# Attention and gated MLP on one core: the Y heads' tokens rotated by 64 partitions and loaded in three transfers, so that sums and values of X and Y heads stand in the same columns

## The chip, the cores and the metric

The kernel runs on one core of a Trainium2 chip. The metric is the device time of one execution in microseconds (us). Before the change, eight executions have a median of 317.72 us, between 315.1 and 320.2.

The engines are named as the profile names them: PE is TensorE's matmul and PEld its weight load, DVE is VectorE, ACT is ScalarE, POOL is GpSimd, SP is SyncE. SP has no arithmetic here; it issues transfers. A name with a q (SPq, POOLq) is an engine's queue.

## The reference

There are 8 batches of 12 heads, 448 tokens and 64 elements a head. Attention comes first, and its output, the heads side by side (768 wide), goes into a gated MLP that mixes tokens.

```python
def rmsnorm(x, g):
    rms = np.sqrt(np.mean(x * x, axis=-1, keepdims=True) + 1e-06)
    return x / rms * g
q_n, k_n = (rmsnorm(q, g_q), rmsnorm(k, g_k))
scores = scale * np.matmul(q_n, k_n.transpose(0, 1, 3, 2))
attn = softmax(scores)
x = (attn @ v), heads side by side

h = np.maximum(x @ w_in, 0.0)
u, v = h[..., :512], h[..., 512:]
v_n = (v - mean(v)) / np.sqrt(var(v) + 1e-06)
v_s = np.einsum('ts,bsd->btd', w_spatial, v_n) + b_spatial[None, :, None]
out = (u * v_s) @ w_out
```

The last five lines and the line with softmax are shortened here. All inputs and the output are float32; the kernel computes most of its products in bfloat16.

## The kernel before, in words

**Tiling of q, k and v.** A partition is one of 128 rows of on-chip memory. 448 tokens are three and a half times 128. The kernel pairs heads 0 to 5 (the X heads) with heads 6 to 11 (the Y heads), so that two heads fill seven chunks of 128 rows: a q or k tile is 128 partitions x 6 heads x 7 chunks x 64 elements. Of each head, tokens 0 to 383 are the main part (partition p, chunk c holds token 3p + c) and tokens 384 to 447 the tail. An X head has its main part in chunks 0 to 2 and its tail in the lower 64 partitions of chunk 3. A Y head has its tail in the upper 64 partitions of chunk 3 and its main part in chunks 4 to 6. So a batch's q takes four transfers (`load_main` and `load_tail`, lines 94 to 106, each for X and Y), k as many. v is kept per head in four chunks, with the half of chunk 3 that a head does not use set to zero (lines 165 and 166); it is loaded by POOL with four transfers a batch (`load_v`).

**Order of the tokens.** After the transposes the tokens of an X head stand as main, tail, and those of a Y head as tail, main. Scores are made key chunk by key chunk (`scores`), and chunk 3 holds 64 keys of an X head and 64 of a Y head.

**A group.** The three groups g of a batch have four heads each: X heads g and 3 + g, Y heads 6 + g and 9 + g. 24 groups run in order; two of their seven score chunks make a step. In each step ScalarE takes the exponential of both (L358). Squares, their sums, the root and the scaling of q and k (L234, L242, L250 and L251, L261) are made some steps ahead by a table of steps written by hand (`EVEN`, `ODD`, `FIRST`, `todo`). From group 6 on, q and k are transposed by transfers that SP issues (L325), and VectorE then multiplies k by the two weights (`k_scale`, L331).

**Attend.** When a group's exponentials are there, `attend` (line 403) makes three sums on TensorE with `weigh` (L379): part -1 with ones, which are the sums of the exponentials, and parts 0 and 1, the two halves of the 64 value columns. A sum of 4 heads x 32 rows fills 128 partitions of one bank of PSUM, the matmuls' output memory; there are four banks in `ps_w` for these and all MLP sums. X heads are written to columns 64 to 511 of the bank and Y heads to columns 0 to 447, so that both have their main part in columns 64 to 447. The tails are then in different columns for the upper and the lower partitions, which is why whatever reads the bank works in three parts (`PARTS`): the main part on 128 partitions x 384 columns, and two tails of 64 x 64. `recip` (L391, L392) takes the logarithm in these three parts and one exponential of its negative, which gives the reciprocal sums rc. `xt_store` (L401) multiplies each half by rc, again in three parts, into xt, the transposed attention output.

**The MLP** of a batch is cut into pieces of a few matmuls (`unit_v`, `unit_u`, `unit_s`, `unit_o`: L465, L495, L505, L537) that `fill` deals out between the scores, a batch later, so that each step gets an equal share. Their results leave PSUM by VectorE or ScalarE (L434, L436, L440, L442, L509).

**Queues.** Every engine works in the order in which the program gives it its instructions. SP issues all q and k loads after the first few, the DMA transposes and the output stores. In the program each of these transfers waits until the one issued eight before it has landed. For batches from 2 on, the loads are entered into `todo` at steps that line 702 gives; a load waits until the tile of two batches before is free.

Of the kernel before, what the change touches and what calls it, by code (L numbers as in the profile page):

```python
# [12 lines left out]
AF = mybir.ActivationFunctionType  # L13
ALU = mybir.AluOpType
# [5 lines left out]
def kernel(  # L20
# [24 lines left out]
    P = 128  # L45
# [38 lines left out]
    def load_tile(b, i):  # L84
        pl = qb_pools[(b + 1) % 2] if b else first
        t = pl.tile([P, 2 * NG, NCH, D], FP, name="kb" if i else "qb")
        qbs[b, i] = t.rearrange("p h c d -> p h (c d)")
        for g in range(NG):
            x = t.rearrange("p (h g) c d -> p h g c d", g=NG)[:, :, g]
            raw[NG * b + g, i] = x  # L90
            if b == 0 and g == 0:
                raw[0, i, 0], raw[0, i, 1] = x[:, :, 0:4], x[:, :, 4:NCH]

    def load_main(b, i, y, g=None, eng=sync):
        c0 = 256 * y
        hs = slice(0, 6) if g is None else slice(g, 6, NG)
        eng.dma_start(out=qbs[b, i][:, hs, c0:c0 + 192], in_=main((q, k)[i][b][6 * y:6 * y + 6][hs]))

    def load_tail(b, i, y, eng=sync):
        eng.dma_start(out=qbs[b, i][64 * y:64 * y + 64, :, 192:256],  # L100
                      in_=tail((q, k)[i][b][6 * y:6 * y + 6]))

    def load_part(b, i, part):
        if part == 0:
            load_tile(b, i)
        (load_main if part < 2 else load_tail)(b, i, part % 2)

    vts = [const.tile([P, H, 4, D], BF, name=f"vt{i}") for i in range(2)]

    def load_v(b, parts):  # L110
        t = vts[b % 2].rearrange("p h c d -> p h (c d)")
        for i in parts:
            y, hs = i % 2, slice(6 * (i % 2), 6 * (i % 2) + 6)
            if i < 2:
                pool.dma_start(out=t[:, hs, 0:192], in_=main(v[b][hs]))
            else:
                pool.dma_start(out=t[64 * y:64 * y + 64, hs, 192:256], in_=tail(v[b][hs]))

    load_tile(0, 0)
    load_tile(0, 1)  # L120
    load_main(0, 0, 0, 0)
    load_main(0, 1, 0, 0, act)
    load_tail(0, 0, 0)
    load_tail(0, 1, 0, act)
    load_tail(0, 0, 1)
    load_tail(0, 1, 1, act)
# [234 lines left out]
    def et_of(G, i, h):  # L361
        s, a = divmod(NCH * G + i, 2)
        return ets[s][:, 2 * a + h, :]
# [4 lines left out]
    def weigh(G, part):  # L368
        b, g = divmod(G, NG)
        vt = vts[b % 2]  # L370
        ps = ps_w.tile([P, 512], FP, name="ps")
        for r in range(4):
            for l in range(4):
                y, h = divmod(l, 2)
                if part < 0:
                    w = ones_t[:, y, :] if r == 3 else ones
                else:
                    w = vt[:, 3 * l + g, r, 32 * part:32 * part + 32]
                pe.matmul(out=ps[32 * l:32 * l + 32, 64 - 64 * y:64 - 64 * y + S], lhsT=w, rhs=et_of(G, 3 if r == 3 else r + 4 * y, h),  # L379
                          start=(r == 0), stop=(r == 3), tile_position=(0, 32 * l))  # L380
        pst[G, part] = ps


    PARTS = ((slice(0, P), slice(64, S), slice(0, SM)), (slice(0, 64), slice(S, 512), slice(SM, S)),
             (slice(64, P), slice(0, 64), slice(SM, S)))

    def recip(G):
        rc = r_pool.tile([P, S], FP, name="rc")
        ps = pst.pop((G, -1))
        for r, i, o in PARTS:  # L390
            act.activation(out=rc[r, o], in_=ps[r, i], func=AF.Ln, bias=0.0, scale=1.0)  # L391
        act.activation(out=rc, in_=rc, func=AF.Exp, bias=0.0, scale=-1.0)  # L392
        rec[G] = rc

    def xt_store(G, half):
        b, g = divmod(G, NG)
        if g == 0 and half == 0:
            xts[b] = x_pool.tile([P, 6, S], BF, name="xt")
        ps = pst.pop((G, half))
        for r, i, o in PARTS:  # L400
            dve.tensor_tensor(out=xts[b][r, 2 * g + half, o], in0=ps[r, i], in1=rec[G][r, o], op=ALU.mult)  # L401

    def attend(G):
        for part in (-1, 0, 1):
# [225 lines left out]
    def early(p):  # L630
        if p == 0:
            transpose_first(0, 1, dve)
            transpose_first(1, 1, dve)
            reduce(1, 0)
        elif p == 3:
            rstd(1)
            scaled(1, 0, eng=dve)
            scaled(1, 1, eng=dve)
            after((1, 1))
            load_v(0, range(4))  # L640
# [24 lines left out]
        if 10 <= p <= 13:  # L665
            attend_late(0, p - 10)
        if 15 <= p <= 18:
            attend_late(1, p - 15)
        if p in (0, 1, 2, 3, 4, 7, 8, 9, 14):
            dummies(6)  # L670
# [29 lines left out]
                        todo.setdefault(s, []).append((what, G, i))  # L700
    for b in range(2, B):
        first_q = {2: S0, 3: 16}.get(b, (21 * b - 36) // 2)
        for n in range(4):
            todo.setdefault(first_q + n // 2, []).append(("ld", NG * b, n))
            todo.setdefault(first_q + 2 + (n if b % 2 == 0 and b > 2 else n // 2), []).append(("ld", NG * b, n + 4))

    ORDER = ("red", "rstd", "sc", "sq", "turn", "tr", "ks", "ld")

    def prep(s, early_act):
        for what, G, i in sorted(todo.get(s, ()), key=lambda x: (ORDER.index(x[0]), x[1:])):  # L710
            if (what == "rstd") != early_act:
                continue
            if what == "ld":
                load_part(G // NG, *divmod(i, 4))
            elif what == "turn":
                transpose_pe(G, i, dve)
            elif what == "sq":
                squares(G, i, eng=act if (G, i) in ((6, 1), (7, 1)) else None)
            elif what == "red":
                reduce(G, i)  # L720
            elif what == "rstd":
                rstd(G)
            elif what == "sc":
                scaled(G, i, eng=dve if (G, i) in ((4, 0), (5, 0)) else None)
            elif what == "tr":
                transpose_dma(G, i)
            elif what == "ks":
                k_scale(G)
# [16 lines left out]
    for s in range(S0, NST):  # L745
        scores(pss[:, 0:2], 2 * s)
        scores(pss[:, 2:4], 2 * s + 1)
        prep(s, True)
        expo(pss, 2 * s, 2)
        prep(s, False)  # L750
        flush()
        if s in v_step:
            load_v(*v_step[s])
        if s == 11:
            load_v(1, range(4))
        if s == 13:
            load_w_sp()
        if s == 21:
            load_w_out()
        if s in gate_step:  # L760
            b = gate_step[s]
            gated(b)
            nxt = min(x for x in list(gate_step) + [NST] if x > s)
            n = sum(1 for x in range(s, nxt - 1) if x not in busy)
            rate = sum(w[0] for w in work) / (n + 0.5)
        if s in busy:
            attend([G for G in range(NGT) if attend_step(G) == s][0])
            quota[0] = 0
        else:
            quota[0] = 0 if s + 1 in busy else 1  # L770
            fill(rate)
# [45 lines left out]
```

## Time and profile before

| what | value |
|---|---|
| median of 8 executions | 317.72 us (315.1 to 320.2) |
| profiled execution, its own time | 316.79 us |
| its span | 315.0 us |
| mean granted clock of TensorE | 0.973 of full speed |
| transfers | 97058 packets, 49.99 MB, mean 159 GB/s |
| the page's chain that ended last | PE 35%, DVE 22%, ACT 15%, POOL 11%, DMA 8%, issue 7% |

The page and the other views come from one execution. Busy time is the time in which an engine had an instruction under way. In the views by group, "idle before" is what the engine stood still ahead of these instructions, and the arrow names what ended most of it. The chain that ended last is followed back from the last instruction, at each step to what released it; "issue" in it is time for which the profile shows no wait. TensorE's matmuls overlap, so a busy TensorE is not one at its peak.

Two figures on transfers: a q or k load of a main part is 576 KB and of a tail 96 KB; their median time from issue to landing is 6.1 us and 5.7 us for q, 7.4 us and 6.0 us for k.

### The profile page before, as it was taken

Reading aid. Unit: us, or ns where it says so; the run is one execution under the profiler, and the core shown is the slowest. Engines: PE = TensorE matmul, PEld = TensorE weight load, DVE = VectorE, ACT = ScalarE, POOL = GpSimd, SP = SyncE. Lnnn points to the kernel's source line nnn. Section 1 sums busy time; section 2 is a strip of 40 time slices with the busy share of each in tenths; the row PEclk is TensorE's granted clock in tenths of the full one; section 3 lists DMA queues with packets and bytes.
Section 4 is the critical chain, followed back from the end, with each engine's and each line's share of the span. In section 5 each row is a group of like instructions: output and inputs, shape, how many; then the busy total and the mean of one; then the engine's idle time right before and its main releaser. Section 6 shows DMA issues by size and latency. Waiting matters only on the chain.

```text
span 315.0 us, 6518 instructions
## 1 busy us (share of the span) xinstructions
PE 277.5 (88%) x2541; PEld 125.9 (40%) x2541; DVE 225.4 (72%) x456; ACT 213.0 (68%) x308; POOL 198.1 (63%) x177
## 2 busy tenths in 40 slices
PE   7488878888969999889988999889989998899995
PEld 7244333433324344334333343334333343444552
DVE  3865866978588759868868958958967956755552
ACT  2678966885758877766867787586777786564411
POOL 3349599589983997469765996399658930400310
PEclk9789979996999999999999999999999999999999
DMA  7989999539999699949899499939530891121135
GB/s 192 323 188 158 257 208 141 155 57 207 166 208 225 155 211 238 284 56 192 145 240 215 45 210 289 220 61 238 88 65 20 83 225 50 27 100 52 25 152 176
DMA packets 97058, 49.99 MB, mean 159 GB/s; under 512 B 66562, under 2 KB 93379, under 8 KB 97027
## 3 DMA queue, kind: packets, MB, share of 16 engines
q1 hardware_dynamic: 74258, 40.71, 56.2%
q0 software_dynamic: 21424, 8.27, 24.2%
q10 hardware_dynamic: 1344, 0.59, 0.7%
q8 instruction: 20, 0.33, 0.5%
q14 instruction: 12, 0.09, 0.1%
HBM read 38.55 MB, written 11.01 MB: 157 GB/s over the span
## 4 chain that ended last, share of the span: by engine, by line
PE 35%; DVE 22%; ACT 15%; POOL 11%; DMA 8%; issue 7%; SPq 1%; ACTq 0%; POOLq 0%; DVEq 0%
ACT et L358 9%; PE ps L537 9%; PE ps L505 6%; DVE xt L401 6%; PE ps L465 5%; PE pss L351 5%; POOL sqt L234 5%; PE ps L379 5%; DVE ms L242 4%; DMA kb<-in_k_dram 4%; POOL n L261 3%; DVE s L473 3%; DMA w_out<-in_moe_w_out_dram 3%; ACT rc L391 2%; PE ps L495 2%
## 5 line engine op out<-in xcount | busy, mean ns | idle before, releaser
L358 ACT ACTIVATE et<-pss 128x1792 bf16<-128x1792 f32 x74 | 123.0, 1662 | 44.9 <-PE pss L351 43.3
L401 DVE TENSOR_TENSOR xt<-ps,rc 128x384 bf16<-128x384 f32 x144 | 43.6, 330 | 46.2 <-ACT rc L392 44.7
L242 DVE TENSOR_REDUCE ms<-sqt 128x14 f32<-128x896 f32 x46 | 49.4, 1077 | 9.5 <-POOL sqt L234 9.0
L537 PE MATMUL ps<-w_out,gt 128*128 128x384 bf16 (+1 forms) x256 | 49.6, 328 | 4.6 <-DVE osb L442 1.9
L465 PE MATMUL ps<-w_in_v,xt 128*128 128x512 bf16 (+1 forms) x192 | 47.6, 381 | 1.5 <-DVE xt L401 1.2
L351 PE MATMUL pss<-qT,kT 64*128 64x448 bf16 x254 | 38.2, 361 | 10.7 <-ACT et L358 5.8
L379 PE MATMUL ps<-et,vt 128*32 128x448 bf16 x768 | 42.7, 360 | 2.5 <-ACT rc L391 2.5
L495 PE MATMUL ps<-xt,w_in_u 128*128 128x448 bf16 x192 | 40.6, 353 | 2.4 <-DVE osb L442 1.8
L261 POOL TENSOR_TENSOR n<-kb,rs 128x896 bf16<-128x896 f32 x22 | 38.6, 1755 | 4.1 <-issue 3.3
L483 POOL TENSOR_SCALAR nm<-mv 128x4 f32<-128x4 f32 x8 | 1.8, 223 | 62.5 <-DVE mv L474 53.0
L261 POOL TENSOR_TENSOR n<-qb,rs 128x896 bf16<-128x896 f32 x18 | 30.5, 1693 | 13.8 <-ACT rs L251 12.7
L234 POOL TENSOR_TENSOR sqt<-qb 128x896 f32<-128x896 f32 x21 | 36.1, 1722 | 0.1
L234 POOL TENSOR_TENSOR sqt<-kb 128x896 f32<-128x896 f32 x21 | 35.4, 1684 | 0.6 <-DMA kb<-in_k_dram 0.5
L537 PEld LDWEIGHTS <-gt 128*128 128x128 bf16 (+1 forms) x256 | 23.4, 100 | 26.1 <-issue 8.6
L442 DVE COPY osb<-ps 128x384 f32<-128x384 f32 (+1 forms) x50 | 26.6, 554 | 8.7 <-PE ps L537 7.8
L505 PE MATMUL ps<-w_spT,vn 128*128 128x448 bf16 (+1 forms) x128 | 29.1, 371 | 0.7 <-DVE xt L401 0.5
L379 PEld LDWEIGHTS <-vt 128*32 128x32 bf16 x768 | 20.9, 99 | 19.8 <-issue 5.7
L487 POOL TENSOR_SCALAR vn<-vs,nm,rv 128x512 bf16<-128x512 bf16 (+1 forms) x32 | 24.1, 766 | 6.1 <-ACT rv L482 3.6
L351 PEld LDWEIGHTS <-kT 64*128 64x128 bf16 x276 | 10.6, 94 | 41.0 <-issue 29.0
L465 PEld LDWEIGHTS <-xt 128*128 128x128 bf16 (+1 forms) x192 | 17.1, 100 | 23.7 <-issue 6.5
L495 PEld LDWEIGHTS <-w_in_u 128*128 128x128 bf16 x192 | 17.2, 98 | 23.1 <-issue 9.3
L473 DVE BATCH_NORM_STATS2 s<-vs 128x6 f32<-128x512 bf16 (+1 forms) x32 | 21.7, 679 | 1.0 <-ACT vs L434 0.8
(85 smaller groups left out, 334.3 us busy)
## 6 DMA issues: line engine op xcount, KB each, us to landing
out_dram<-osb SPq DMA_DIRECT2D x24, 384.0 KB, 4.9
qb<-in_q_dram SPq DMA_DIRECT2D x14, 576.0 KB, 6.1
kb<-in_k_dram SPq DMA_DIRECT2D x14, 576.0 KB, 7.4
vt<-in_v_dram POOLq DMA_DIRECT2D x16, 288.0 KB, 5.7
qb<-in_q_dram SPq DMA_DIRECT2D x16, 96.0 KB, 5.7
kb<-in_k_dram SPq DMA_DIRECT2D x14, 96.0 KB, 6.0
out_dram<-osb SPq DMA_DIRECT2D x7, 192.0 KB, 4.0
qb<-in_q_dram SPq DMA_DIRECT2D x6, 192.0 KB, 4.6
```

Of the source, the lines that this page charges most:

```text
L234: pool.tensor_tensor(out=t, in0=x, in1=x, op=ALU.mult)
L242: dve.tensor_reduce(out=sqs[gk][:, key[1], :], in_=sqt.pop(key).rearrange("p h c d -> p (h c) d"), axis=AX.X, op=ALU.add)
L261: (eng or pool).tensor_tensor(out=t.rearrange("p c h d -> p h c d"), in0=raw[key], in1=rst[gk][:, key[1], :].rearrange("p (h c) -> p h c", ...
L351: pe.matmul(out=ps[:, h, 0:S], lhsT=kT[r, c0:c0 + 128], rhs=qT[r, :], start=True, stop=True, tile_position=(64 * h, 0))
L358: act.activation(out=ets[s][:, 2 * a:2 * a + 2 * m, :], in_=ps[:, 0:2 * m, 0:S], func=AF.Exp, bias=0.0, scale=1.0)
L379: pe.matmul(out=ps[32 * l:32 * l + 32, 64 - 64 * y:64 - 64 * y + S], lhsT=w, rhs=et_of(G, 3 if r == 3 else r + 4 * y, h), start=(r == 0), ...
L401: dve.tensor_tensor(out=xts[b][r, 2 * g + half, o], in0=ps[r, i], in1=rec[G][r, o], op=ALU.mult)
L465: pe.matmul(out=ps[0:m, :], lhsT=xts[b][:, j, t0:t0 + m], rhs=w_in_v[:, j, :], start=(j == 0), stop=(j == 5), tile_position=(0, 0))
L473: dve.bn_stats(out=s6[0:m, :], in_=vs[b][c][0:m, :])
L495: pe.matmul(out=ps[:, 0:S], lhsT=w_in_u[:, j, 128 * f:128 * f + 128], rhs=xts[b][:, j, :], start=(j == 0), stop=(j == 5))
L505: pe.matmul(out=ps[:, 0:S], lhsT=vn_t[b % 2][0:kp, c, 128 * f:128 * f + 128], rhs=w_spT[0:kp, c, :], start=(c == 0), stop=(c == NT - 1))
L537: pe.matmul(out=ps[o:o + m, 0:384], lhsT=gts[b][f][:, t0:t0 + m], rhs=w_out[:, f, r], start=(f == 0), stop=(f == 3), tile_position=(0, o))
```

## The change

The Y heads' tokens are turned by 64 partitions. In chunk 3 the upper 64 partitions now hold the first 64 rows of the main part's first column of tokens, and each later chunk holds the other half of one column and the first half of the next; the tail ends up in the upper half of chunk 6. Read chunk after chunk, the tokens of a Y head thus stand in the same order as those of an X head: main, tail. A Y head's main part takes two transfers of 64 partitions, so a tensor takes five transfers in place of four; bytes and run lengths stay. v is loaded in the same way and its Y heads use the lower zeros in chunk 0.

All sums are written to columns 0 to 447, so `PARTS` goes: `recip` makes one logarithm in place of three, and `xt_store` one product for each half in place of three. The steps of the loads are laid out anew for five parts (q and k one after the other, three or four in a step), and the v loads of a batch are spread over five steps in place of four.

```diff
-    def load_main(b, i, y, g=None, eng=sync):
-        c0 = 256 * y
-        hs = slice(0, 6) if g is None else slice(g, 6, NG)
-        eng.dma_start(out=qbs[b, i][:, hs, c0:c0 + 192], in_=main((q, k)[i][b][6 * y:6 * y + 6][hs]))
...
+    def pieces(x):
+
+        m, t = main(x), tail(x)
+        return ((slice(0, P), 0, 3, m), (slice(0, 64), 3, 1, t), (slice(64, P), 0, 3, m[0:64]),
+                (slice(0, 64), 1, 3, m[64:P]), (slice(64, P), 3, 1, t))
+
+
+    def load_part(b, i, part, g=None, eng=sync):
+        if part == 0 and (b, i) not in qbs:
             load_tile(b, i)
-        (load_main if part < 2 else load_tail)(b, i, part % 2)
+        y, hs = int(part > 1), slice(0, 6) if g is None else slice(g, 6, NG)
+        r, c, n, x = pieces((q, k)[i][b][6 * y:6 * y + 6][hs])[part]
+        c += 3 * y
+        eng.dma_start(out=qbs[b, i][r, hs, D * c:D * (c + n)], in_=x)
...
+            hs = slice(6, 12) if i > 1 else slice(0, 6)
+            r, c, n, x = pieces(v[b][hs])[i]
+            pool.dma_start(out=t[r, hs, D * c:D * (c + n)], in_=x)
+
+    load_part(0, 0, 0, 0)
+    load_part(0, 1, 0, 0, act)
+    load_part(0, 0, 1)
+    load_part(0, 1, 1, None, act)
+    load_part(0, 0, 2, 0)
+    load_part(0, 1, 2, 0, act)
     act.preload_act_table_set("natural_log_exp_and_others")
-    load_main(0, 0, 1, 0)
-    load_main(0, 1, 1, 0, act)
+    load_part(0, 0, 3, 0)
+    load_part(0, 1, 3, 0, act)
+    load_part(0, 0, 4)
+    load_part(0, 1, 4, None, act)
     for g in (1, 2):
         for i in (1, 0):
-            load_main(0, i, 0, g)
-            load_main(0, i, 1, g)
-    for n in range(8):
-        load_part(1, *divmod(n, 4))
+            for part in (0, 2, 3):
+                load_part(0, i, part, g)
+    for n in range(10):
+        load_part(1, *divmod(n, 5))
...
-        dve.memset(t[0:64, 6:12, 3, :], 0.0)
+        dve.memset(t[0:64, 6:12, 0, :], 0.0)
...
-                    w = vt[:, 3 * l + g, r, 32 * part:32 * part + 32]
-                pe.matmul(out=ps[32 * l:32 * l + 32, 64 - 64 * y:64 - 64 * y + S], lhsT=w, rhs=et_of(G, 3 if r == 3 else r + 4 * y, h),
+                    c = (3, 0)[y] if r == 3 else r + y
+                    w = vt[:, 3 * l + g, c, 32 * part:32 * part + 32]
+                pe.matmul(out=ps[32 * l:32 * l + 32, 0:S], lhsT=w, rhs=et_of(G, 3 if r == 3 else r + 4 * y, h),
...
-        for r, i, o in PARTS:
-            act.activation(out=rc[r, o], in_=ps[r, i], func=AF.Ln, bias=0.0, scale=1.0)
+        act.activation(out=rc, in_=pst.pop((G, -1))[:, 0:S], func=AF.Ln, bias=0.0, scale=1.0)
...
-        for r, i, o in PARTS:
-            dve.tensor_tensor(out=xts[b][r, 2 * g + half, o], in0=ps[r, i], in1=rec[G][r, o], op=ALU.mult)
+        dve.tensor_tensor(out=xts[b][:, 2 * g + half, :], in0=pst.pop((G, half))[:, 0:S], in1=rec[G],
+                          op=ALU.mult)
...
-        for n in range(4):
-            todo.setdefault(first_q + n // 2, []).append(("ld", NG * b, n))
-            todo.setdefault(first_q + 2 + (n if b % 2 == 0 and b > 2 else n // 2), []).append(("ld", NG * b, n + 4))
+        for n in range(10):
+            todo.setdefault(first_q + n // (3 if b > 2 else 4), []).append(("ld", NG * b, n))
...
-            v_step.update({s + 6 + i: (b + 2, [i]) for i in range(4)})
+            v_step.update({s + 6 + i: (b + 2, [i]) for i in range(5)})
```

More of the change, by code (lines that the diff above doesn't have):

```diff
@@ L92, in load_tile @@
                 raw[0, i, 0], raw[0, i, 1] = x[:, :, 0:4], x[:, :, 4:NCH]
-    def load_main(b, i, y, g=None, eng=sync):
-        c0 = 256 * y
-        hs = slice(0, 6) if g is None else slice(g, 6, NG)
-        eng.dma_start(out=qbs[b, i][:, hs, c0:c0 + 192], in_=main((q, k)[i][b][6 * y:6 * y + 6][hs]))
[L99 to L104, printed above, removed]
+    def pieces(x):
[4 more added lines that the diff above has]
+        if part == 0 and (b, i) not in qbs:
             load_tile(b, i)
-        (load_main if part < 2 else load_tail)(b, i, part % 2)
+        y, hs = int(part > 1), slice(0, 6) if g is None else slice(g, 6, NG)
+        r, c, n, x = pieces((q, k)[i][b][6 * y:6 * y + 6][hs])[part]
+        c += 3 * y
+        eng.dma_start(out=qbs[b, i][r, hs, D * c:D * (c + n)], in_=x)
     vts = [const.tile([P, H, 4, D], BF, name=f"vt{i}") for i in range(2)]
@@ L112, in load_v @@
         for i in parts:
[L113 to L126, printed above, removed]
+            hs = slice(6, 12) if i > 1 else slice(0, 6)
[7 more added lines that the diff above has]
+    load_part(0, 1, 2, 0, act)
     act.preload_act_table_set("natural_log_exp_and_others")
-    load_main(0, 0, 1, 0)
-    load_main(0, 1, 1, 0, act)
+    load_part(0, 0, 3, 0)
+    load_part(0, 1, 3, 0, act)
+    load_part(0, 0, 4)
+    load_part(0, 1, 4, None, act)
     for g in (1, 2):
         for i in (1, 0):
-            load_main(0, i, 0, g)
-            load_main(0, i, 1, g)
-    for n in range(8):
-        load_part(1, *divmod(n, 4))
+            for part in (0, 2, 3):
+                load_part(0, i, part, g)
+    for n in range(10):
+        load_part(1, *divmod(n, 5))
     ident = const.tile([P, P], BF)
@@ L377, in weigh @@
                 else:
-                    w = vt[:, 3 * l + g, r, 32 * part:32 * part + 32]
-                pe.matmul(out=ps[32 * l:32 * l + 32, 64 - 64 * y:64 - 64 * y + S], lhsT=w, rhs=et_of(G, 3 if r == 3 else r + 4 * y, h),
+                    c = (3, 0)[y] if r == 3 else r + y
+                    w = vt[:, 3 * l + g, c, 32 * part:32 * part + 32]
+                pe.matmul(out=ps[32 * l:32 * l + 32, 0:S], lhsT=w, rhs=et_of(G, 3 if r == 3 else r + 4 * y, h),
                           start=(r == 0), stop=(r == 3), tile_position=(0, 32 * l))
         pst[G, part] = ps
-    PARTS = ((slice(0, P), slice(64, S), slice(0, SM)), (slice(0, 64), slice(S, 512), slice(SM, S)),
-             (slice(64, P), slice(0, 64), slice(SM, S)))
     def recip(G):
         rc = r_pool.tile([P, S], FP, name="rc")
-        ps = pst.pop((G, -1))
-        for r, i, o in PARTS:
-            act.activation(out=rc[r, o], in_=ps[r, i], func=AF.Ln, bias=0.0, scale=1.0)
+        act.activation(out=rc, in_=pst.pop((G, -1))[:, 0:S], func=AF.Ln, bias=0.0, scale=1.0)
         act.activation(out=rc, in_=rc, func=AF.Exp, bias=0.0, scale=-1.0)
@@ L398, in xt_store @@
             xts[b] = x_pool.tile([P, 6, S], BF, name="xt")
-        ps = pst.pop((G, half))
-        for r, i, o in PARTS:
-            dve.tensor_tensor(out=xts[b][r, 2 * g + half, o], in0=ps[r, i], in1=rec[G][r, o], op=ALU.mult)
+        dve.tensor_tensor(out=xts[b][:, 2 * g + half, :], in0=pst.pop((G, half))[:, 0:S], in1=rec[G],
+                          op=ALU.mult)
     def attend(G):
@@ L639, in early @@
             after((1, 1))
-            load_v(0, range(4))
+            load_v(0, range(5))
             load_w_in(1)
@@ L713, in prep @@
             if what == "ld":
-                load_part(G // NG, *divmod(i, 4))
+                load_part(G // NG, *divmod(i, 5))
             elif what == "turn":
@@ L754 @@
         if s == 11:
-            load_v(1, range(4))
+            load_v(1, range(5))
         if s == 13:
```

## The prediction

> **What bounds the kernel now.** I read the page's busy times first. No engine is at its limit over the whole span, TensorE comes nearest:
>
> ```profile
> PE 277.5 (88%) x2541; PEld 125.9 (40%) x2541; DVE 225.4 (72%) x456; ACT 213.0 (68%) x308; POOL 198.1 (63%) x177
> ```
>
> From 126 us on the kernel repeats every two batches (68.5 us), so I asked next for busy time by stretch, cut where the chain of waits changes its engine. Columns: stretch, its length, busy us (instructions) of PE, PEld, DVE, ACT, POOL, clock, DMA share, GB/s.
>
> ```profile
> 104.00:126.65 22.65, 21.73 (x216) 8.94 (x208) 17.09 (x33) 17.64 (x26) 20.18 (x15) 1.00 1.10 199
> 126.65:144.50 17.85, 15.22 (x128) 6.37 (x127) 13.16 (x30) 12.76 (x19) 11.53 (x11) 1.00 0.74 153
> 144.50:171.40 26.90, 24.48 (x217) 10.26 (x221) 22.70 (x46) 18.17 (x25) 19.09 (x17) 1.00 1.04 214
> 171.40:195.10 23.70, 23.01 (x240) 9.99 (x238) 17.47 (x34) 18.83 (x26) 21.65 (x16) 1.00 0.93 169
> ```
>
> TensorE idles 2.63 us in the second line, 2.42 in the third, 0.69 in the fourth: the last is bound by TensorE, the two before it are not. The chain of waits (start, us, what) says by what:
>
> ```profile
> 162.69 0.48 ACT rc L391 x2
> 163.16 0.01 issue
> 163.18 0.23 ACT rc L391
> 163.41 0.02 issue
> 163.43 0.58 ACT rc L392
> ...
> 164.04 0.68 DVE xt L401 x2
> 164.72 0.01 issue
> 164.73 0.23 DVE xt L401
> ...
> 169.75 1.07 DVE kT L331 x2
> 170.83 0.05 issue
> 170.87 0.55 PE pss L351 x4
> ```
>
> VectorE takes its work in order. It waits for the reciprocal sums of a head group, then scales the two halves of the result, then does what is queued behind: copies, sums of squares, and the k scaling (L331) on which the next scores (L351) depend. Each attend is thus a serial piece ScalarE, VectorE, TensorE. What it consists of, grouped by form (line, engine, operation, tiles, shapes, count | busy us, mean ns | idle before):
>
> ```profile
> L401 DVE TENSOR_TENSOR xt<-ps,rc 128x384 bf16<-128x384 f32 x48 | 26.7, 557 | 45.5 <-ACT rc L392 44.7
> L401 DVE TENSOR_TENSOR xt<-ps,rc 64x64 bf16<-64x64 f32 x96 | 20.8, 217 | 0.7
> ...
> L391 ACT ACTIVATE rc<-ps 128x384 f32<-128x384 f32 x24 | 11.6, 485 | 0.8 <-PE ps L379 0.8
> ...
> L391 ACT ACTIVATE rc<-ps 64x64 f32<-64x64 f32 x48 | 10.3, 215 | 0.3
> ```
>
> A 64x64 piece has a sixth of the columns of a main piece and costs 0.4 of its time; there are two for each main piece.
>
> [...] The trace has no engine count, but 64-partition loads land in 5.7 to 6.0 us against 6.1 to 7.4 for the 576 KB ones[...].
>
> **The change part by part.**
>
> *Scaling (L401).* Each half: two 64x64 pieces go, the main piece grows from 384 to 448 columns. Price of a 128x448 product from PSUM: 557 + 64 x 1.06 = 625 ns; the row of gt (L509, same shape) has 620. 48 x (557 + 2 x 217 - 620) = 17.8 us of VectorE busy. The timeline shows the six of an attend in 1.88 us; two of gt stand there in 1.16 to 1.2. So 0.68 us an attend.
>
> *Logarithm (L391).* Three become one of 448 columns: 485 + 64 x 0.84 = 538 ns, which is also the mean of us (L434, same shape). The three take 0.81 us in the timeline, so 0.27 us an attend; 24 x (485 + 430 - 538) = 9.0 us of ScalarE busy.
>
> Both lie one behind the other: up to 0.95 us for each of 24 attends.
>
> *Steady part, 104 to 287 us.* In 126.65 to 144.5 one attend is fully on the chain and a second for half of its scaling, after which TensorE is late: I take 1.2 us of the 2.63 idle. In 144.5 to 171.4 two attends are on it, 1.9 us; the idle is 2.42, and behind the VectorE chain stand waits that do not get shorter (sums of squares from POOL to VectorE to ScalarE's logarithm, L250), so 1.4. In the TensorE stretch 0.2. Together 2.8 of 68.5 us, 7.5 us over 183 us. The stretch 104 to 126.65 shows that TensorE runs at 96% at best (21.73 of 22.65); I take four fifths: **-6.0 us**, bounds -2 and -10.
>
> *Matmuls.* Counts, widths and order are the same on TensorE; the write begins at column 0 of the bank in place of 0 or 64. No row shows a cost for that; I take nothing.
>
> *Loads on SP.* A tensor takes five transfers in place of four (batch 0: three for each later group in place of two), bytes and runs unchanged. In the steady part each issue is 0.6 to 0.7 us of SP, and each transfer waits for the eighth before it. SP waits 89 us for POOL's n before transposes, so there is room. Behind the loads stand the DMA transposes of q and k and the stores. For k the smallest gap I found between landing and use is 3.4 us (issued at 181.91, 5.4 us to land, used by L331 at 190.70); two more issues are 1.3 us, 2.6 with their waits. Cost nothing; if the gap is used up, see the rivals.
>
> *k loads moved one to two steps earlier.* For batch 3 the first, largest k piece goes ahead of two transposes that kept it back until 72.06 us. Chain there: k landed at 81.3, POOL's squares waited 0.55 us for it, and w_out, issued by POOL at 83.92, kept TensorE waiting 1.49 us at 91.95. Four v pieces ahead of w_out cost 0.93 + 3 x 0.70 in place of 3.2 us. So w_out leaves 0.7 us earlier, and up to 0.65 more from the scaling at 58 us, where VectorE is 97% busy. With four attends in 57 to 104: **-1.5 us**, bounds 0 and -4. The far end has the clock drop in it: at 72 to 74 us TensorE worked 0.70 of 2 us, partly waiting for xt (0.75 and 0.55), and ran at 0.50 until 80. Ten matmuls at 0.39 in place of 0.19 us and two score groups at 0.93 in place of 0.55 are 2.7 us that a shorter wait may spare. I do not count on it.
>
> *Start, 0 to 57 us.* The first piece of work needs 98 KB of long runs in place of 98 KB of short ones: 0.3 us earlier. The q loads of group 1 come behind three more issues and the eight-deep limit: landed at 10.6 us, now about 12.4, where ScalarE takes them at 11.39. That is 1 us on ScalarE, but VectorE's n at 13.92 waits behind a sum until then anyway: nothing, at most +1. POOL issues a fifth v piece: 895 ns for the 128-partition piece, 703 for each 64-partition one with 384 runs, so 895 + 4 x 703 against 2 x 895 + 2 x 703, +0.51 us each. At 21.6 us it moves the last v piece from about 28.5 to 29.2, where TensorE starts on v at 28.27: +0.6. At 47 us POOL is busy without a gap: +0.5. The two attends there give back 0.3. Start: **+0.8 us**, bounds -0.4 and +2.2. Later v pieces lie beside POOL's idle time (15.5 us of waits for rs, mv and ps between 126.65 and 195.1).
>
> *End.* After 287.3 us TensorE waits for the last xt, 0.86 us on its weight load. The scaling ends 0.95 us earlier, TensorE then has its own earlier matmuls to finish: **-0.4 us**, bounds -0.2 and -0.9.
>
> Sum: -6.0 - 1.5 + 0.8 - 0.4 = -7.1 us. The profiled execution took 316.79 us (span 315.0 and 1.8 around it), which gives 309.7; the median of the eight runs is 0.93 above that execution, which gives 310.6. I say **310.0**.
>
> **Rivals.**
> *Smaller, TensorE takes over at once:* the stretches with 91% busy TensorE may hold hidden waits inside the modelled matmul ends. For it: 171.4 to 195.1 and 104 to 126.65 are TensorE's already. Against it: 5 us of idle in each 68.5. Then -2 in the steady part and nothing at 57 to 104: 317 - 1.6 = 315.5.
> *Larger:* most of the 0.95 us counts at 20 attends, and the clock drop goes. -10 - 4 + 0.5 - 0.5 gives 303.
> *Slower, the SP queue:* ten transfers a batch in place of eight, eight in flight, smaller ones. At batches 5 and 7 nine loads stand before a q transpose, at 4 and 6 three; a load that waits for a lane holds transposes and stores behind it. It decides once the k transposes come over 3.4 us later: then kT is late, then the scores, then ScalarE's exponentials. At 2 us past that for each of the six batches: +12 - 8 = +4, 321. For it: the two k loads at 192.69 already took 2.51 us to issue. Against it: SP has nothing to do from 169 to 179 us, and mostly waits for POOL before a q transpose.
>
> **How the numbers follow.** Main case 0.60 (307 to 313.5), smaller 0.20 (313.5 to 318), larger 0.09 (302 to 307), slower 0.11. A measurement of this kernel tells 0.5%, 1.6 us, from no change. Of the smaller case 0.09 falls within that, so faster 0.80, same 0.09, slower 0.11. The range 304 to 316.5 leaves out the slower case, most of the no-change case and the far end of the larger one.
>
> **What would show it.** L401 with 48 instructions near 620 ns and L391 with 24 near 538; VectorE busy near 208 us, ScalarE near 204; the period of two batches near 66 us; TensorE idle less in the VectorE stretches and not in its own; POOL's v issues up by about 4 us in all. Wrong: k scaling or scores waiting for a transpose; TensorE waiting for v near 28 us by over 1 us; VectorE's wait for rc growing by what the scaling saves, which would mean that the slot was only moved.

## The result and the profile after

The changed kernel takes **312.96 us** (median of 11 runs, 312.21 to 316.35) against 318.12 us (median of 32 runs, 315.1 to 321.55) for the kernel before; the ratio is 0.9868 with a 95% interval of 0.9836 to 0.9901. Some executions of a kernel fall into a slower state, and this ratio, like every one below, leaves them out, so it is not the quotient of the medians. The forecast was 310.0 with a range of 304 to 316.5. The kernel became faster, as said, by 5.2 us between the medians and by 4.2 us by the ratio (1.32% of 318.12), where 7.7 were forecast. Between the two profiled executions the span went from 315.0 to 311.0 us, which is 4.0 us where the sum of the steps had 7.1.

First the page's row of busy times, of the changed kernel:

```profile
PE 278.6 (90%) x2541; PEld 129.1 (42%) x2541; DVE 208.6 (67%) x360; ACT 205.9 (66%) x260; POOL 202.0 (65%) x185
```

VectorE has 96 instructions and 16.8 us less, ScalarE 48 instructions and 7.1 us less; TensorE has the same 2541 instructions (278.6 in place of 277.5 us). The groups by form show the merged instructions at their forecast prices (620 and 538 ns), and the two that touch v:

```profile
L393 DVE TENSOR_TENSOR xt<-ps,rc 128x448 bf16<-128x448 f32 x48 | 27.9, 618 | 42.3 <-ACT rc L386 37.4 <-PE ps L379 4.8
...
L385 ACT ACTIVATE rc<-ps 128x448 f32<-128x448 f32 x24 | 12.9, 538 | 0.8 <-PE ps L379 0.8
...
L116 POOL DMA_DIRECT2D vt<-in_v_dram x40 | 29.3, 739 | 0.0
...
L379 PE MATMUL ps<-et,vt 128*32 128x448 bf16 x768 | 46.3, 379 | 5.2 <-DMA vt<-in_v_dram 3.5 <-ACT rc L385 1.7
```

POOL's v issues went from 25.5 to 29.3 us in all, as forecast. The last row holds the first surprise: TensorE waited 3.5 us for v. In the kernel before, v was not among what it waited for there:

```profile
L379 PE MATMUL ps<-et,vt 128*32 128x448 bf16 x768 | 42.7, 360 | 2.5 <-ACT rc L391 2.5
```

Next the stretches of two batches, cut at the same reciprocals as the three stretches that the prediction shows (126.65 to 195.10 there). Columns: stretch, length, busy us (instructions) of PE, PEld, DVE, ACT, POOL, clock, DMA share, GB/s.

```profile
130.65:147.40 16.75, 15.07 (x137) 6.88 (x130) 12.26 (x22) 12.14 (x17) 11.28 (x11) 1.00 1.06 182
147.40:172.70 25.30, 23.86 (x213) 10.01 (x211) 20.88 (x36) 17.78 (x21) 19.71 (x18) 1.00 1.06 193
172.70:195.93 23.23, 22.69 (x238) 10.09 (x236) 16.21 (x27) 18.05 (x20) 22.28 (x17) 1.00 1.10 198
```

The period is 65.28 us in place of 68.45. The three stretches are shorter by 1.10, 1.60 and 0.47 us; TensorE's idle time in them went from 2.63, 2.42 and 0.69 to 1.68, 1.44 and 0.54. That is 2.08 of the 3.17 us; the other 1.09 come off TensorE's busy time with the same work, which suggests that some waiting had been counted as busy (the profile models the ends of matmuls: 16 of L379 stand in 0.94 us, at a median of 353 ns for one). The chain of waits (start, us, what) at the same place as in the prediction says why:

```profile
162.74 1.66 ACT et L357
164.41 0.44 ACT rc L385
164.85 0.04 issue
164.89 0.94 PE ps L379 x16
165.83 0.31 PE pss L346 x4
```

In the kernel before, the chain went from the logarithm through the reciprocal into six scalings on VectorE. Now it goes from the logarithm back to TensorE's matmuls. The page's chain says it for the whole span: TensorE's share rose from 35% to 50%, VectorE's fell from 22% to 11%, ScalarE's from 15% to 9%; SP's issues rose from 1% to 2%.

Where the rest went is seen best by following one instruction through the run. The table takes the start of the reciprocal's exponential for a few head groups (G1 is the second of 24), as its offset in us against the same instruction of the kernel before, all read from the timelines of single executions. Experiments described below stand in it too.

| run | G1 | G3 | G7 | G11 | G15 | G19 | G23 |
|---|---|---|---|---|---|---|---|
| changed kernel | +4.64 | +5.13 | +4.65 | +2.45 | +0.82 | -2.01 | -3.92 |
| e1, all in three parts | +4.76 | +5.25 | +3.74 | +3.77 | +3.79 | +3.82 | +3.84 |
| e2, split by partitions only | +4.35 | +4.36 | +4.56 | +4.59 | +4.61 | +4.64 | +4.66 |
| e3, v issued early | +4.18 | +4.67 | +3.09 | +0.88 | -0.75 | -3.59 | -5.51 |
| e7, logarithm in three parts | +5.37 | +5.86 | +4.60 | +2.83 | +1.74 | -0.29 | -1.91 |
| e8, products in three parts | +4.45 | +4.95 | +4.21 | +3.24 | +2.72 | +1.62 | +1.07 |
| e9, batch 0 as before | +0.71 | +0.94 | -0.30 | -2.52 | -4.14 | -6.98 | -8.90 |
| e11, split by heads only | +0.30 | +0.31 | -0.47 | -0.48 | -0.49 | -0.52 | -0.54 |

The changed kernel loses 4.64 us before its second head group and gains 8.57 us from G7 to G23, evenly (3.2 us in each period of two batches). After G23 both kernels take the same (27.7 and 27.6 us). The start's loss is no accident of one execution: G1 stands at +4.18 to +5.37 in the six kernels of the table that split batch 0's Y parts of q and k by partitions, and at +0.30 to +1.12 in those that do not (e9, e11 and, outside the table, e6).

The loss at the start shows in the windows. The kernel before:

```profile
5.00:10.00 5.00, 2.47 (x40) 2.28 (x38) 2.30 (x5) 1.88 (x5) 1.04 (x1) 1.00 1.12 300
10.00:15.00 5.00, 3.00 (x26) 1.49 (x27) 4.13 (x8) 3.67 (x7) 1.81 (x2) 0.68 1.11 327
15.00:20.00 5.00, 5.00 (x44) 3.10 (x43) 2.47 (x4) 2.93 (x5) 1.81 (x2) 0.63 1.16 273
20.00:25.00 5.00, 3.33 (x37) 1.88 (x35) 4.66 (x6) 4.33 (x7) 3.48 (x6) 1.00 0.70 96
```

The changed kernel:

```profile
5.00:10.00 5.00, 2.57 (x40) 2.38 (x38) 2.54 (x5) 2.19 (x5) 1.04 (x1) 1.00 0.98 224
10.00:15.00 5.00, 2.96 (x29) 1.67 (x30) 4.02 (x9) 3.46 (x6) 2.05 (x4) 0.71 0.65 170
15.00:20.00 5.00, 5.00 (x43) 2.91 (x41) 2.54 (x4) 3.24 (x7) 1.61 (x1) 0.61 0.92 220
20.00:25.00 5.00, 3.50 (x41) 2.04 (x38) 4.46 (x6) 4.32 (x6) 3.67 (x7) 1.00 1.16 242
```

Read the last two columns, the busy share of the transfer engines (the time that packets took; at 1.11 and 1.16 some of them overlap) and GB/s. Most of the loads came at 300, 327 and 273 GB/s in the first 20 us; now they come at 224, 170 and 220 and fill the next five microseconds as well. Between 10 and 15 us the share fell too, from 1.11 to 0.65: there the engines in part had nothing to do. From 21.4 us on POOL issues batch 0's v. How long its pieces took from issue to landing, in the kernel before:

```profile
DMA to landing us min/median/max: 4.4/4.6/5.2
```

and in the changed kernel:

```profile
DMA to landing us min/median/max: 7.9/8.1/8.3
```

The timeline of the changed kernel has what follows (start, us, engine, line, what, and in brackets the wait ahead of it and its releaser):

```profile
29.75 0.37 PE L379 MATMUL ps<-et,vt 128*32 128x448 bf16 x2 [1.61 <-DMA vt<-in_v_dram]
...
32.00 1.20 PE L379 MATMUL ps<-et,vt 128*32 128x448 bf16 x14 [1.89 <-DMA vt<-in_v_dram]
```

ScalarE's next exponential, behind these matmuls, waits 6.74 us. That raises two questions: is the gain the merged instructions alone, and what about the loads is slow?

### The profile page after: what moved, and what is told of

It is laid out like the page before. It is cut to its first block, busy times and chain, and to the rows that moved or that the text cites. A ratio compares the mean times of both kernels' runs of the same rounds, so it can differ in the third digit from the quotient of the medians.

```text
span 311.0 us, 6419 instructions
## 1 busy us (share of the span) xinstructions
PE 278.6 (90%) x2541; PEld 129.1 (42%) x2541; DVE 208.6 (67%) x360; ACT 205.9 (66%) x260; POOL 202.0 (65%) x185
## 4 chain that ended last, share of the span: by engine, by line
PE 50%; POOL 13%; DVE 11%; ACT 9%; DMA 7%; issue 6%; SPq 2%; POOLq 0%; DVEq 0%
PE ps L379 11%; PE ps L458 10%; PE ps L530 9%; PE ps L498 7%; PE pss L350 7%; ACT et L357 6%; POOL sqt L233 5%; POOL n L260 3%; PE ps L488 3%; DMA vt<-in_v_dram 3%; POOL vn L480 2%; DVE ms L241 2%; SPq L107 2%; DVE s L466 2%; POOL vt L116 2%
## 5 line engine op out<-in xcount | busy, mean ns | idle before, releaser
L393 DVE TENSOR_TENSOR xt<-ps,rc 128x448 bf16<-128x448 f32 x48 | 27.9, 618 | 42.3 <-ACT rc L386 37.4
L379 PE MATMUL ps<-et,vt 128*32 128x448 bf16 x768 | 46.3, 379 | 5.2 <-DMA vt<-in_v_dram 3.5
L530 PE MATMUL ps<-w_out,gt 128*128 128x384 bf16 (+1 forms) x256 | 47.6, 327 | 1.7 <-DVE osb L435 1.4
L458 PE MATMUL ps<-w_in_v,xt 128*128 128x512 bf16 (+1 forms) x192 | 46.6, 381 | 0.0
L530 PEld LDWEIGHTS <-gt 128*128 128x128 bf16 (+1 forms) x256 | 24.2, 100 | 21.9 <-issue 8.6
L379 PEld LDWEIGHTS <-vt 128*32 128x32 bf16 x768 | 22.5, 103 | 24.3 <-issue 8.0
L116 POOL DMA_DIRECT2D vt<-in_v_dram x40 | 29.3, 739 | 0.0
L498 PE MATMUL ps<-w_spT,vn 128*128 128x448 bf16 (+1 forms) x128 | 28.4, 364 | 0.3 <-DVE w_spT L209 0.3
L350 PEld LDWEIGHTS <-kT 64*128 64x128 bf16 x276 | 10.2, 94 | 40.5 <-issue 28.2
L458 PEld LDWEIGHTS <-xt 128*128 128x128 bf16 (+1 forms) x192 | 17.8, 100 | 19.3 <-issue 5.1
```

Source lines behind the costliest of these rows:

```text
L116: pool.dma_start(out=t[r, hs, D * c:D * (c + n)], in_=x)
L350: pe.matmul(out=ps[:, h, 0:S], lhsT=kT[r, c0:c0 + 128], rhs=qT[r, :], start=True, stop=True, tile_position=(64 * h, 0))
L379: pe.matmul(out=ps[32 * l:32 * l + 32, 0:S], lhsT=w, rhs=et_of(G, 3 if r == 3 else r + 4 * y, h), start=(r == 0), stop=(r == 3), tile_posi ...
L458: pe.matmul(out=ps[0:m, :], lhsT=xts[b][:, j, t0:t0 + m], rhs=w_in_v[:, j, :], start=(j == 0), stop=(j == 5), tile_position=(0, 0))
L498: pe.matmul(out=ps[:, 0:S], lhsT=vn_t[b % 2][0:kp, c, 128 * f:128 * f + 128], rhs=w_spT[0:kp, c, :], start=(c == 0), stop=(c == NT - 1))
L530: pe.matmul(out=ps[o:o + m, 0:384], lhsT=gts[b][f][:, t0:t0 + m], rhs=w_out[:, f, r], start=(f == 0), stop=(f == 3), tile_position=(0, o))
```

## The experiments

**The merged instructions undone (e1).** All loads as in the changed kernel, logarithm and products in three parts again, at the new columns. The medians of the kernel before beside these runs were 317.6 to 318.7 us, so the ratios can be compared.

```diff
+    PARTS = ((slice(0, P), slice(0, SM)), (slice(0, 64), slice(SM, S)), (slice(64, P), slice(SM, S)))
...
-        act.activation(out=rc, in_=pst.pop((G, -1))[:, 0:S], func=AF.Ln, bias=0.0, scale=1.0)
+        for r, o in PARTS:
+            act.activation(out=rc[r, o], in_=ps[r, o], func=AF.Ln, bias=0.0, scale=1.0)
...
+        for r, o in PARTS:
+            dve.tensor_tensor(out=xts[b][r, 2 * g + half, o], in0=ps[r, o], in1=rec[G][r, o], op=ALU.mult)
```

> The changed kernel, but the logarithm and both products are made in three parts again, now at the same columns (0 to 383, and two 64x64 tails). Theory A, the steady gain is the merged instructions: the 8.6 us that the changed kernel gains between the second and the last attend go back, 321 to 322 us. Theory B, the gain comes from the k loads that are issued earlier: at most 2 us go back, 313 to 315.

Measured: 322.05 us, ratio 1.0104 (1.0045 to 1.0163). In the table its offset hardly changes between G7 and G23 (+3.74 to +3.84). So the whole steady gain is the merged instructions, and the new loads alone make the kernel slower.

**One of the two merges alone (e7, e8).** The same edit for the logarithm only, and for the products only.

> The changed kernel with only ScalarE's logarithm in three parts again. By the prediction's terms (0.27 us of 0.95 an attend) it gives back 0.28 of the 9 us: 315 to 316 us. If the steady part is bound by VectorE alone, nothing: 313.

> The changed kernel with only VectorE's products in three parts again. By the prediction's terms (0.68 us of 0.95 an attend) it gives back 0.72 of the 9 us: 319 to 320 us. If only the latency up to the first half counts, about 316.

Measured: 314.87 us, ratio 0.9932 (0.9901 to 0.9964), with the logarithm in three parts; 319.14 us, ratio 1.0061 (1.0032 to 1.0091), with the products in three parts. Against the changed kernel that is 1.9 and 6.2 us, about 1 to 3 (2.1 and 5.4 us in the table, from G7 to G23); the prediction had 0.27 and 0.68 us an attend, 1 to 2.5. Each is worth some third of its full price: 24 x 0.27 = 6.5 us and 24 x 0.68 = 16.3 us.

**The loads alone (e2).** The kernel before, with each Y main part of q and k loaded in two transfers of 64 partitions. Columns, sums and v stay.

```diff
+        x = main((q, k)[i][b][6 * y:6 * y + 6][hs])
+        for r in (slice(0, 64), slice(64, P)) if y else (slice(0, P),):
+            eng.dma_start(out=qbs[b, i][r, hs, c0:c0 + 192], in_=x[r])
```

> The kernel before, only that each q and k load of a Y head's main part is issued as two transfers of 64 partitions; no rotation, v as before. Theory A, more and smaller transfers on SP in the first 20 us push the loads of batch 1 into those of v: the second attend comes 3.5 to 5 us later, 321.5 to 323.5 us. Theory B, the start is lost by v's fifth transfer and its queue on POOL: no change, 317.5 to 318.5.

Measured: 323.59 us (four executions, 321.7 to 327.6), ratio 1.0139 (1.0054 to 1.0225). The offset is +4.35 us at G1 and +4.66 at G23. So the split costs its 4.4 us in the start, and the extra loads of all later batches cost 0.3 us together. In this kernel, then, SP has room in the steady part, which speaks against the prediction's slower rival.

**v ahead of the crowd (e3, e4).** The call that issues batch 0's v is moved up, right behind the second square of head group 1: in the changed kernel (e3) and in the kernel before (e4).

```diff
     squares(1, 1)
+    load_v(0, range(5))
...
-            load_v(0, range(5))
             load_w_in(1)
```

> The changed kernel with batch 0's five v transfers issued by POOL right behind its second square (at about 12.7 us) in place of 21.5. Theory A, TensorE's wait for v between 28 and 32 us is what the start loses, the rest follows from it: that wait goes, the second attend is 4.5 us earlier, 307 to 309 us. Theory B, the other things at 28 to 32 us (POOL's weight load queue, k of group 2) hold it as well: 311 to 313.

> The kernel before with the same move of batch 0's v loads. Theory A, v was in time there: 317 to 319 us. Theory B, an earlier v speeds the start of any layout: 314 or less.

Measured: e3 311.13 us, ratio 0.9772 (0.9703 to 0.9842); e4 319.38 us, ratio 1.003 (0.9996 to 1.0063), no change that can be told. The wait for v goes in e3, yet G1 still stands at +4.18. The timeline of e3 has the reason:

```profile
36.20 1.68 POOL L233 TENSOR_TENSOR sqt<-kb 128x896 f32<-128x896 f32 x1 [7.66 <-DMA kb<-in_k_dram]
```

Now batch 1's k is late. So v's place is not the cause: the loads of the start together take longer, and here the order only chose who waits. What e3 gains against the changed kernel comes mostly after G3 (+4.67 to +3.09 at G7, where the changed kernel goes from +5.13 to +4.65).

**Some of the k loads issued by POOL (e5, e6).** If SP's issuing were the limit, a second issuer would help. The k loads of head groups 1 and 2 of batch 0 are given to POOL: in the changed kernel (e5, six transfers) and in the kernel before (e6, four).

```diff
     for g in (1, 2):
-        for i in (1, 0):
-            for part in (0, 2, 3):
-                load_part(0, i, part, g)
+        for part in (0, 2, 3):
+            load_part(0, 0, part, g)
...
+    for part in (0, 2, 3):
+        load_part(0, 1, part, 1, pool)
...
+    for part in (0, 2, 3):
+        load_part(0, 1, part, 2, pool)
```

> The changed kernel with the six k transfers of batch 0's groups 1 and 2 issued by POOL, which is idle then (2.8 to 6.5 and 7.5 to 10 us), in place of SP. Theory A, SP's 0.63 us for each of its transfers is what keeps the DMA engines half idle at 10 to 15 us: SP is through with batch 1 some 4 us earlier, v and k of batch 1 both land in time, the second attend is 4 us earlier, 305.5 to 308.5 us. Theory C, the DMA engines themselves are slower on the 64-partition pieces: it stays at 311 to 313.

> The kernel before with the same k transfers (four there) issued by POOL. Theory A, SP was not late there: 316.5 to 319 us. Theory C: the same. Only if this alone gains 3 us or more is the gain of the changed kernel with it no repair of its start.

Measured: e5 314.11 us, ratio 0.9868 (0.9832 to 0.9903), which is the changed kernel's; e6 320.24 us, ratio 1.0091 (1.0041 to 1.0141). e5 brought nothing (theory C had 311 to 313 us), and e6 was slower by 0.9%, which no theory had. The window of e5 where the changed kernel had a share of 0.65 and 170 GB/s:

```profile
10.00:15.00 5.00, 2.67 (x22) 1.62 (x22) 3.99 (x9) 3.34 (x9) 3.44 (x5) 0.79 1.10 196
```

With a second issuer the transfer engines were busy again and still moved only some 200 GB/s (e2 has 1.15 and 213 GB/s between 5 and 10 us). That spoke against SP as the only limit and for something in the transfers themselves.

**Batch 0 as before (e9), batches 0 and 1 as before (e10).** The rotated order begins with batch 1 or with batch 2; the batches ahead of it keep the old loads, columns and three parts. As the zeros of v stand in another chunk for the two orders, POOL zeroes chunk 0 of a v buffer once more when the orders change.

```diff
+    OLD = (0,)
...
+        if b in OLD:
+            return ((slice(0, P), 0, 3, m), (slice(0, 64), 3, 1, t), (slice(0, P), 0, 3, m),
+                    (slice(64, P), 3, 1, t))
...
+        if b - 2 in OLD and 0 in parts:
+            pool.memset(vts[b % 2][0:64, 6:12, 0, :], 0.0)
...
-                    c = (3, 0)[y] if r == 3 else r + y
+                    c = r if b in OLD else (3, 0)[y] if r == 3 else r + y
...
+        for r, i, o in parts_of(G):
+            dve.tensor_tensor(out=xts[b][r, 2 * g + half, o], in0=ps[r, i], in1=rec[G][r, o], op=ALU.mult)
```

> The changed kernel, but batch 0 (q, k, v, its weighing, logarithm and products) in the order and the parts of the kernel before; batches 1 to 7 rotated. Batch 0's q and k need 16 transfers again instead of 22, all of its Y mains on 128 partitions; batch 1 keeps its 20 instead of 16. Column 0 of the first v buffer is zeroed once more by GpSimd ahead of batch 2's v. Theory A (the 4.65 us that the start lost are batch 0's extra and half-as-tall transfers): the reciprocal of group 1 stands at +0 to +1.5 us against the kernel before instead of +4.65, the gain between groups 7 and 23 stays at 8 to 9 us, time 309 to 311 us. Theory B (batch 1's loads, ten transfers instead of eight, run into batch 0's v): group 1 stays at +3 us or more, time 312.5 to 313.5. Theory C (an earlier start is given back by TensorE's halved clock between 50 and 104 us): group 1 at +0 to +1.5, group 7 at +3 or more, time 312 to 313.

> As the run with batch 0 alone in the old order, but batches 0 and 1 both: all 32 q and k transfers of the start and both first v loads are those of the kernel before, attends 0 to 5 work in three parts, and the rotated order begins with batch 2. Theories A and B both: the reciprocals of groups 1 to 5 within 0.7 us of the kernel before, group 23 at -8 to -9.5 us, time 309 to 310.5 us; under A this differs from the run with batch 0 alone by at most 1 us, under B it is 3 us faster than that. Theory C (the start's gain is given back between 50 and 104 us): group 1 near 0, group 7 at +3 or more, time 312 to 313.

Measured: e9 **308.68 us**, ratio 0.9763 (0.9693 to 0.9833); e10 **308.31 us**, ratio 0.9713 (0.9653 to 0.9774). Both beat both kernels, by a little more than was expected. In e9 G1 stands at +0.71 in place of +4.64, and the gain from G7 to G23 is 8.60 us, as in the changed kernel. The window of e9 where the changed kernel had 170 GB/s, and its one wait for v:

```profile
10.00:15.00 5.00, 3.08 (x28) 1.61 (x29) 4.06 (x9) 3.56 (x6) 1.94 (x3) 0.70 1.14 298
```

```profile
29.00 0.93 PE L392 MATMUL ps<-et,vt 128*32 128x448 bf16 x14 [0.49 <-DMA vt<-in_v_dram]
```

So the start's loss is that of batch 0's transfers (theory A). Theory C fell too: G7 stands at -0.30. Batch 1's two extra ones (ten in place of eight; the counts of batch 1 and of the start in the two expectations are too high) cost nothing that these runs can tell: e9 and e10 differ by 0.4 us, within their ranges. Of e10 only the times are used here.

**Number or height (e11).** e2 changed two things: more transfers, and transfers that reach 64 partitions only. e11 is the kernel before with exactly as many transfers and as many bytes in each as e2, but split by heads, so that each reaches all 128 partitions.

```diff
+        if y == 0:
+            both = (hs,)
+        elif g is None:
+            both = (slice(0, 3), slice(3, 6))
+        else:
+            both = (slice(g, g + 1), slice(g + 3, g + 4))
+        for r in both:
+            eng.dma_start(out=qbs[b, i][:, r, c0:c0 + 192], in_=x[:, r])
```

> The kernel before with as many q and k transfers as in the run that split the Y main parts by partitions, and as many bytes in each, but split by heads: two transfers on all 128 partitions with half the heads each. Nothing else is changed. Theory A1 (the start is lost to the number of transfers: SP issues one at a time and only eight are in flight): the reciprocal of group 1 at +3.5 to +5 us as in that run (+4.35), about 200 GB/s between 10 and 15 us, time 321.5 to 323.5 us. Theory A2 (it is lost to transfers that reach 64 partitions only, which take SP and the transfer engines longer for their bytes): group 1 at 0 to +1.5 us, close to 300 GB/s between 10 and 15 us, issues of 0.4 us in place of 0.63, time 318 to 319.5 us.

Measured: 318.54 us, ratio 1.0006 (0.9973 to 1.004), and +0.30 us at G1. The number of transfers alone costs 0.3 us at G1; the 64 partitions, on top of it, cost the other 4.05. Where it sits, the timeline of SP's queue shows for the same 96 KB half of a Y part. e2, by partitions:

```profile
6.81 0.59 SPq L99 DMA_DIRECT2D kb<-in_k_dram  x1
```

e11, by heads:

```profile
6.72 0.33 SPq L105 DMA_DIRECT2D kb<-in_k_dram  x1
```

SP is held 0.59 us in place of 0.33 by the issue. A larger load need not hold it longer: the kernel before issues one of 576 KB on 128 partitions in 0.37 us (at 28.77 us), though two others there (at 72.06 us) take 0.58 each. And the transfer engines need longer for the bytes, as the window from 5 to 25 us shows for e2:

```profile
5.00:25.00 20.00, 14.76 (x153) 10.06 (x151) 14.25 (x22) 14.10 (x25) 9.35 (x13) 0.91 1.04 220
```

and for e11:

```profile
5.00:25.00 20.00, 13.78 (x140) 8.84 (x137) 13.57 (x21) 13.14 (x22) 8.26 (x11) 0.83 1.02 250
```

The engines are as busy (1.04 and 1.02), but move 220 GB/s in one and 250 in the other; the kernel before has 249 in that window at 1.02. Over 20 us 30 GB/s are 0.6 MB, which at 250 GB/s take 2.4 us. One expectation was too narrow: I wrote close to 300 GB/s between 10 and 15 us, and it was 243.

The larger number was not free in itself; there was room for it. SP's last two issues of batch 1's k, in the kernel before, in e11 and in e2:

```profile
15.57 2.38 SPq L100 DMA_DIRECT2D kb<-in_k_dram  x2
19.41 1.31 SPq L108 DMA_DIRECT2D kb<-in_k_dram  x2
20.79 1.36 SPq L102 DMA_DIRECT2D kb<-in_k_dram  x2
```

They end at 17.95, 20.72 and 22.15 us, and batch 0's v, issued behind them or among them, takes a median of 4.6, 5.5 and 9.1 us to land. In e11 it is still in time. Whether the split by partitions would cost as much with fewer transfers was not run.

From 5 to 25 us the changed kernel moved 214 GB/s. That is a little less than e2, but its transfer engines were also less busy there (0.93). No run holds the lower rate of the transfer engines apart from SP's longer issue, so how much each costs stays open, and so does why 64 partitions make either of them slower.

## Why the prediction was right or wrong

**The prices of the merged instructions: right.** 618 and 538 ns, where 620 and 538 were forecast. The forecast's 1.06 and 0.84 ns an element are the differences of the rows before over 320 columns, (557 - 217) / 320 and (485 - 215) / 320. In all VectorE was busy for 208.6 us and ScalarE for 205.9, where near 208 and near 204 were forecast. No row of the changed kernel shows a cost for the new columns (the matmuls of L379 have a median of 353 ns, before 352).

**The steady part: right in mechanism, too small.** Measured -8.57 us from G7 to G23, forecast -6.0. Two terms were mis-sized. The prediction summed 1.2, 1.4 and 0.2 us to 2.8 us a period; the stretches gave 1.10, 1.60 and 0.47, together 3.17. The third, TensorE's own, was the one most off. Then it took four fifths of 7.5 us because TensorE would be at 96% at best, an estimate from one stretch (its own table has 23.01 of 23.70 us, 97%, in another); that discount was wrong. 3.17 of 68.45 us over the 182 us from G7 to G23 are 8.4 us, nothing was taken off, and TensorE still idles 3.66 us in each period.

**The k loads moved earlier: a third of it.** Forecast -1.5 us for 57 to 104 us, which is from G3 to G7; measured -0.48 (+5.13 to +4.65). In e1, e3 and e9 the same stretch gains 1.5, 1.6 and 1.2 us, so the size may be right. But e2 and e11, whose loads stand where the kernel before has them, lose 0.2 and gain 0.8 there, so single executions do not settle it. One thing that differs is the clock, as the page's rows show, the kernel before first:

```profile
PEclk9789979996999999999999999999999999999999
```

and the changed kernel:

```profile
PEclk9779798899669999999999999999999999999999
```

Cut finer, into windows of 0.8 us, TensorE ran at half clock (0.50 granted) after the first 20 us for 10.2 us before, in pieces of 3.4 and 6.8 us, and for 20.5 us now, in three of 3.4 us and one of 10.2. The first of the pieces now begins at 32.5 us, 0.5 us after TensorE's second wait for v ended (32.00). That the rest of the gain went there is possible and not shown: no run held the clock alone, and e9 had some 14 us at half clock after the first 20 us, more than the kernel before, and gained. (That is an estimate from its mean clock, 0.966 over 306.0 us, and the 0.83 of its window from 5 to 25 us.)

**The start: wrong, and this is the step that failed.** Forecast +0.8 us for 0 to 57 us with a bound of +2.2, measured +5.13 at G3, of which +4.64 stand at G1. The prediction said that POOL's fifth issue "moves the last v piece from about 28.5 to 29.2, where TensorE starts on v at 28.27: +0.6", and gave the q loads of group 1 "nothing, at most +1", counting three more issues. Both terms count issues and take the transfers as fast as before. For that its only measured ground was that 96 KB tails land in 5.7 to 6.0 us. The landing times did not show the rate: the 288 KB q loads took a median of 6.5 us in e2 and 6.4 in e11, while the loads of the start moved at 220 and 250 GB/s. e11 against e2 shows that the count alone costs next to nothing and the height on top of it 4.05 us at G1 (+4.35 against +0.30). In the start the loads come onto the path once their room is used up (SP's last issue of batch 1's k ended at 22.15 us in e2 and at 17.95 before, and v took 9.1 us to land in place of 4.6); in the steady part the same transfers are covered (e2: 0.3 us from G1 to G23). The sign that the prediction had named for its failure, over 1 us of wait for v near 28 us, is what the profile shows (1.61 and 1.89). One small term was right: the first piece of work came earlier, with VectorE's first sums of squares at 7.57 in place of 7.82 us, where 0.3 us were forecast; whether longer runs or the new order of the issues did that, no run shows.

**The end: nearly nothing.** Forecast -0.4, measured -0.1.

Together: +5.13 - 0.48 - 8.57 - 0.08 = -4.00 us, the difference of the spans. The forecast's -7.1 differs from it by 4.3 us in the start, 1.0 in the second term and 0.3 at the end, less 2.6 us of underrated gain. That the forecast came as near as it did is luck in part: two errors had opposite signs.

**The rivals.** The smaller one (TensorE takes over at once, -2 in the steady part) fell: the steady part gave 8.57, and the time of 313 us lies near this rival's only because of the start. The larger one (-10 there, and the clock drop gone) did not come either: the time at half clock after the first 20 us grew from 10.2 to 20.5 us. The slower one, SP's queue behind more loads, did not show in e2 and e11, whose extra loads in the steady part cost 0.3 us and nothing.

## What to carry to other kernels

Before splitting a transfer, ask whether the pieces still reach all partitions: halves by partitions cost 4.4 us in the start of this kernel, halves by another dimension 0.3. What is nearly free in a steady part that hides its loads (e2: 0.3 us from G1 to G23) may be dear in a start that waits for them (4.35 us up to G1); the two deserve separate layouts, and here the mixed version (308.3 to 308.7 us) beats both uniform ones. A merge of small instructions on a serial chain is worth what it takes off that chain where the chain decides, not the busy time it saves: here 8.6 us from G7 to G23, where the two engines lost 23.9 us of busy time in all.

## What the runs showed of the hardware

- A load issue of 96 KB held SP for 0.59 us where it reached 64 partitions and for 0.33 us where it reached 128 (e2 and e11, same bytes, same place in the queue); issues of 576 KB on 128 partitions held it for 0.37 us and for 0.58 us (the kernel before, at 28.77 and 72.06 us).
- With the transfer engines equally busy (1.04 and 1.02), the loads of the start moved at 220 GB/s with the split by partitions (e2, 5 to 25 us) and at 250 GB/s with the split by heads (e11).
- Landing times show it for some loads only: the 288 KB k loads took a median of 7.8 us in e2 and in the changed kernel, 6.5 us in e11; the 288 KB q loads 6.5, 6.3 and 6.4 us.
